# Value products of two neighbouring tiles in one run, in the second batch of an attention and feed-forward kernel

## The chip, the cores and the metric

The kernel runs on one core of one Trainium2 chip. Its time is that of one execution on the device, in microseconds (us); the number compared is the median of several runs. Before the change three runs gave 717.25, 718.96 and 721.09 us, a median of 718.96. One more execution was profiled, and every row below is of that one: it took 717.12 us, of which 715.3 us lie between the first and the last instruction of the program (the span).

A core has a matrix engine (PE, whose weight loads are shown apart as PEld), a vector engine (DVE), a scalar engine (ACT), a general engine (POOL) and a sync engine (SP) that here issues nearly all DMAs. Each engine takes its own instructions strictly in order.

## The reference

Three steps follow each other: attention in which a query sees only the keys of its own hash bucket, a feed-forward layer with x * sigmoid(x), and a second one with x - tanh(x). All in 32 bits.

```python
# q, k, v: (2, 8, 768, 64); proj: (64, 6)
q_bits = (np.einsum('bhsd,dk->bhsk', q, proj) > 0)       # k_bits likewise
q_bucket = np.sum(q_bits * 2 ** np.arange(6), axis=-1)   # k_bucket likewise
mask = q_bucket[:, :, :, None] == k_bucket[:, :, None, :]
scores = np.where(mask, scale * q @ k.T, -1e9)
attn = np.exp(scores - max); attn = attn / (sum + 1e-09)
x = (attn @ v), heads side by side                       # (1536, 512)
h = x @ w_in;   x = (h * sigmoid(h)) @ w_out             # 512 -> 2048 -> 512
h = x @ w_in2;  out = (h - tanh(h)) @ w_out2             # 512 -> 2048 -> 512
```

## The kernel before

**Attention.** There are 2 batches of 8 heads, and a head has 6 tiles of 128 queries against all 768 keys: 96 tiles, 48 of each batch. For each head q and k are split into a high and a low part (`q_hi`, `k_hi`, `q_lo`, `k_lo`; the low part of q is line L420, that of k L427) so that two short-format products give a 32-bit one; a product with `proj` (the hash, L454) gives the bucket bits, which are written into spare rows of the same operands, so that the scores come out masked. A tile then goes this way: four score matmuls (L658, `ps<-k,q`), the maximum on DVE (L662), the bias (L667) and the exponential on ACT (L672), a high half in 16 bits (L354, `hl<-p`) and a low half on POOL (L726, `hl<-p,hl`), one transposing DMA for both (L729, `pt<-hl`), and the value products: 18 matmuls of 65 columns (L750 to L752), for each of 6 key tiles high by high, high by low and low by high, all accumulated in one bank. Some tiles of the first batch are transposed on PE instead (L686), and seven of those use one 32-bit product (L744). When all 6 tiles of a head are done the result is divided by the sums (L773 to L781) and transposed (L793). The values v are scaled and split per pair of heads (L554 to L590, the helpers `copy` L354 and `scaled` L358 and L360).

**Feed-forward.** The hidden layer is done in four chunks of 512. Weights come as 64-bit words and are converted to 32 bits by ACT, POOL and DVE (first layer L1061 to L1083, second L1386 to L1401), then split in high and low. L1143 are the matmuls into the hidden layer, L1147 the tanh, L1151 the gate, L354 `gh` and L1158 its two halves, L1221 the matmuls out of it and L1226 to L1232 the accumulation. The first batch's tokens go through the first layer while the second batch's attention still runs: from about 124 us on PE alternates between score tiles, value products and groups of twelve feed-forward matmuls of 384 columns. After that comes the first layer for the second batch (16-bit operands, with weights read back from DRAM, L944 to L996), and then the second layer for all tokens, with seven products in place of eight (L1565, groups of six, with L1576 and L1582 putting them together, the gate in L1606 to L1616, the matmuls out of the hidden layer in L1656 and their accumulation in L1661 and L1663).

**What sets the order.** No instruction is issued where it is written. Every piece of work is handed to a planner (`Plan.add`) with the engines that may do it, an assumed cost on each, a key (roughly the moment at which it is due), the pieces that it depends on and the buffers that it takes. `Plan.order` then runs a list schedule: on each engine it takes, among the pieces that could start soonest, the one with the lowest key, and where several engines may do a piece a number `b_...` says how much later the first of them may be before the other is taken (50 or more: always the first). All these numbers stand in the table `KNOBS`. Pieces with the same `line` keep their sequence: score tiles `s`, value products `pv`, transposing DMAs `pt`, and sets of weight buffers `wset`. The value products of a tile get their key from `K["pv"]`; the list `two` already allows two tiles to be put into one piece, when `twos` is set and the batch is the second. The transposed probabilities have four buffers (`pt_slots`).

Of the kernel before, what the change touches and what calls it, by code (L numbers as in the profile page):

```python
# [25 lines left out]

KNOBS = dict(b_ysc=2.96, b_wsc=0.38, convw=36.631, cw=6, cjw=3.488, stt=0.005, hold_w2=20, twos=0, start=1.292,
             step=1.908, gap=9.852, step1=3.658, ffn=3.795, ffn3=2.276, pv=10.67, prep=15.957, hash=20.15,
             slack=0.056, conv=34.353, conv0=81.24, vld=4.608, vmax=5.066, vsplit=11.76, x2=0.165, direct=0.354,
             direct1=0, b_qh=100, b_qlo=2.34, b_kup=100, b_vlo=100, b_bi=100, b_thi=100, b_shi=100, b_slo=100,  # L30
             b_xh=2.01, b_xlo=100, b_wlo=100, b_clip=2.73, b_hhi=1.34, k_m=0.1, k_e=0.334, k_t=2.024, k_th=2.717,
             k_tl=1.55, k_hi=1.446, k_lo=1.897, k_f=2.576, cj=3.28, cl=7.627, ahead=2, emode=1, lmode=1, xsets=0,
             raws=8, vmax1=24.884, ffn2=1.46, xprep=20.673, xprep1=2.231, xk1=4.211, convo=55.136, convh=107.674,
             fill=8.355, convo0=43.254, convh0=58.847, fill0=36.161, plain=3, cj2=3.475, half=2, b_xph=2.35,
             b_xpl=100, b_cl2=2.82, b_wl2=100, b_sh=100, b_ss=100, b_u3=100, b_hh2=1.21, b_hl2=0.01, by=2.442,
             by2=7.875, parts=5.995, wend=46.5, b_part=2.81, vst1=5.174, vgap=6.028, vl=15.282, vsp=2.176,
             whole=0.17, chunk=0, b_kh=100, b_vh=0.38, b_vs=-0.33, b_whi=100, hold_r=30.482, hold_v=11.313,
             hold_v1=23.734, hold_w=10.65, hold_o=49.111, near=2)

# [169 lines left out]
def lsh_attention_moe_kernel(  # L209
# [180 lines left out]
    for n in range(NHEAD):  # L390
# [11 lines left out]
        else:  # L402
            ld = [add("SP", 0.4, lambda raw=raw, b=b, h=h: nc.sync.dma_start(out=get(raw), in_=qkT[b, h]), at - 12,
                      takes=[raw], tail=2.47, hold=at - K["hold_r"] if n > 1 else 0.0)] * 2
# [29 lines left out]
        parts = [qh, kh]  # L434
# [96 lines left out]
    for x in range(B * H // 2):  # L531
# [7 lines left out]
        if x == 0:  # L539
            la, va, hold_v = K["vld"], a0 + K["vmax"], K["hold_v"]  # L540
# [348 lines left out]
    for ps_i, (e, fresh, blks) in enumerate(PASSES):  # L889
# [4 lines left out]
        for c, fc in enumerate(chunks):  # L894
# [3 lines left out]
            for m in range(2):  # L898
# [114 lines left out]
                for j in range(fc if m else KD):  # L1013
# [77 lines left out]
                    else:  # L1091
# [5 lines left out]
                    x = add(("ACT", "POOL"), c2(0.62, 0.62), w_hi, kj + 2.5, [a] + prior[:1],  # L1097
                            takes=[held] if j == 0 else [], uses=[wa] + ([held] if j else []), give="whi")
                    y = add(("POOL", "DVE"), c2(1.29, 0.68), w_lo, kj + 3, [x], uses=[wa, held], port=("DVE",), give="wlo")
# [641 lines left out]
```

## Time and profile before

| | |
|---|---|
| runs | 717.25, 718.96, 721.09 us |
| profiled execution | 717.12 us, span 715.3 us |
| PE busy | 692.8 us, 97% of the span |
| DVE, ACT, POOL busy | 578.9 (81%), 481.3 (67%), 464.3 us (65%) |
| chain that ended last | PE 71%, DVE 14%, ACT 9% of the span |
| TensorE clock granted | 0.995 on average, 0.91 in the first 40 us |

Busy is the time in which an engine executes something, with the pipelined parts of consecutive instructions counted once. A matmul's shown duration is longer than the distance to the next one, because they overlap: distances between starts are what a list of matmuls costs. Time in which PE is idle shows only as the difference between a stretch and PE's busy time in it, and a weight load that nothing hides shows as a larger distance between two starts.

### The profile page before, as it was taken

How to read it: one execution, taken by the hardware profiler on the slowest of the kernel's cores; microseconds unless marked ns; L12 is line 12 of the kernel's file. 1: busy time of each engine (PE TensorE's matmuls, PEld its weight loads, DVE VectorE, ACT ScalarE, POOL GpSimd, SP SyncE). 2: the span in 40 equal slices, each digit the busy share in tenths (PEclk: the TensorE clock that was granted, in tenths of full speed). 3: DMA queues.
4: the chain of work that ended last, by engine and by line, in shares of the span. 5: the costliest groups of instructions: out<-in, count | busy, mean ns of one | idle time of the engine just before them, and what ended most of it. 6: DMA issues, size and time to landing. Idle time of an engine off the chain costs nothing.

```text
span 715.3 us, 14275 instructions
## 1 busy us (share of the span) xinstructions
PE 692.8 (97%) x5372; PEld 566.9 (79%) x5372; DVE 578.9 (81%) x1141; ACT 481.3 (67%) x884; POOL 464.3 (65%) x376
## 2 busy tenths in 40 slices
PE   7888899999999999999999999999999999999998
PEld 4777789999999999999655666558697796978977
DVE  5999999798797898778898758996689689786563
ACT  6799999997897896765866554655645546463250
POOL 6799998887688776845439482659855655772010
PEclk9899999999999999999999999999999999999999
DMA  9999998998999999993444004210033014110102
GB/s 326 225 234 246 209 199 178 257 221 198 220 237 267 218 210 230 236 198 97 150 147 158 16 1 133 89 59 1 1 94 127 17 59 122 57 60 1 58 31 89
DMA packets 148249, 101.48 MB, mean 142 GB/s; under 512 B 120668, under 2 KB 129116, under 8 KB 148180
## 3 DMA queue, kind: packets, MB, share of 16 engines
q1 hardware_dynamic: 147812, 100.27, 56.4%
q8 instruction: 42, 0.69, 0.4%
q10 hardware_dynamic: 368, 0.30, 0.1%
q14 instruction: 27, 0.22, 0.1%
HBM read 57.97 MB, written 11.53 MB: 97 GB/s over the span
## 4 chain that ended last, share of the span: by engine, by line
PE 71%; DVE 14%; ACT 9%; issue 3%; DMA 2%; POOL 1%; ACTq 0%; SPq 0%; DVEq 0%; POOLq 0%
PE psm L1656 18%; PE psm L1221 14%; PE psm L1143 12%; PE psm L1565 11%; PE ps L658 7%; ACT p L672 2%; PE pso L750 2%; PE pso L751 2%; PE pso L752 2%; PE ps L454 2%; DVE wcol L944 1%; DVE cv L1397 1%; DVE p L662 1%; ACT p L354 1%; DVE cv L1392 1%
## 5 line engine op out<-in xcount | busy, mean ns | idle before, releaser
L726 POOL TENSOR_TENSOR hl<-p,hl 128x768 f16<-128x768 f32 x75 | 126.0, 1682 | 37.3 <-ACT hl L354 31.7
L1565 PE MATMUL psm<-xoh,ws 128*128 128x384 f16 x448 | 113.2, 327 | 2.5 <-ACT x L1576 2.2
L1221 PE MATMUL psm<-gh,wh 128*128 128x384 f16 (+1 forms) x384 | 107.3, 332 | 0.0
L1565 PEld LDWEIGHTS <-ws 128*128 128x128 f16 x672 | 64.2, 98 | 47.1 <-issue 6.1
L662 DVE TENSOR_SCALAR_CACHE_REDUCE p<-ps 128x768 f32<-128x768 f32 x96 | 90.7, 951 | 12.0 <-PE ps L658 9.7
L658 PE MATMUL ps<-k,q 128*128 128x384 f32 x384 | 90.0, 361 | 6.9 <-DVE p L662 4.1
L672 ACT ACTIVATE p<-p,bi 128x768 f32<-128x768 f32 x96 | 89.8, 941 | 1.5
L1656 PE MATMUL psm<-gh,wh 128*128 128x384 f32 x256 | 88.5, 346 | 0.1
L1656 PE MATMUL psm<-gl,wh 128*128 128x384 f32 x256 | 85.9, 335 | 0.8 <-DVE gl L1616 0.8
L1656 PE MATMUL psm<-gh,wl 128*128 128x384 f32 x256 | 85.8, 335 | 0.0
L1221 PE MATMUL psm<-gl,wh 128*128 128x384 f32 (+1 forms) x256 | 84.7, 331 | 0.0
L658 PEld LDWEIGHTS ps<-k,q 128*128 128x128 f32 x384 | 65.6, 194 | 10.9 <-DVE p L662 7.2
L1565 PE MATMUL psm<-xol,ws 128*128 128x384 f16 x224 | 73.1, 326 | 0.0
L1143 PE MATMUL psm<-x16h,wh 128*128 128x384 f16 x256 | 63.4, 326 | 0.0
L354 ACT CAST hl<-p 128x768 f16<-128x768 f32 x75 | 62.7, 836 | 0.6
L1221 PEld LDWEIGHTS <-wh 128*128 128x128 f16 x384 | 37.4, 98 | 24.6
L1143 PEld LDWEIGHTS <-wh 128*128 128x128 f16 x384 | 37.2, 98 | 24.4
L1663 DVE TENSOR_TENSOR acc<-acc,psm 128x384 f32<-128x384 f32 x48 | 26.3, 550 | 32.8 <-PE psm L1656 32.8
L750 PE MATMUL pso<-v16h,pt 128*128 128x65 f16 x450 | 49.5, 195 | 0.0
L1656 PEld LDWEIGHTS psm<-gh,wh 128*128 128x128 f32 x256 | 48.1, 188 | 1.5 <-DVE acc L1663 0.2
L1656 PEld LDWEIGHTS psm<-gl,wh 128*128 128x128 f32 x256 | 48.1, 188 | 1.5 <-DVE gl L1616 1.5
L751 PE MATMUL pso<-v16l,pt 128*128 128x65 f16 x450 | 48.9, 194 | 0.0
(202 smaller groups left out, 2014.6 us busy)
## 6 DMA issues: line engine op xcount, KB each, us to landing
w<-in_w_in_dram SPq DMA_DIRECT2D x32, 512.0 KB
w<-in_w_out_dram SPq DMA_DIRECT2D x32, 512.0 KB
r<-in_qkT_dram SPq DMA_DIRECT2D x15, 768.0 KB
wi<-wa SPq DMA_DIRECT2D x16, 256.0 KB
wo<-wa SPq DMA_DIRECT2D x16, 256.0 KB
wl<-wi SPq DMA_DIRECT2D x16, 256.0 KB
wl<-wo SPq DMA_DIRECT2D x16, 256.0 KB
vr<-in_v_dram SPq DMA_DIRECT2D x8, 384.0 KB
```

Of the source, the lines that this page charges most:

```text
L354: nc.scalar.copy(out, in_) if e == "ACT" else ENG[e].tensor_copy(out, in_)
L658: nc.tensor.matmul(out=get(ps)[:, u, 0:HS], lhsT=x[:, t * 128:(t + 1) * 128], rhs=c[:, u * HS:(u + 1) * HS], start=(j == 0), stop=(j == 1))
L662: nc.vector.tensor_scalar(get_p().rearrange("p (c s) -> p c s", c=2), get(ps)[:, :, 0:HS], FLOOR, None, op0=ALU.max, op1=ALU.max, accum_ou ...
L672: nc.scalar.activation(out=get_p(), in_=get_p(), func=ACTF.Exp, scale=0.125, bias=get(bi))
L726: ENG[e].tensor_tensor(get_hl()[:, 1, :], get_p(), get_hl()[:, 0, :], op=ALU.subtract)
L750: nc.tensor.matmul(out=o, lhsT=pt[:, kt, :], rhs=v16[:, kt, :], start=(kt == 0), stop=False)
L751: nc.tensor.matmul(out=o, lhsT=pt[:, kt, :], rhs=v16l[:, kt, :], start=False, stop=False)
L1143: nc.tensor.matmul(out=ps, lhsT=a[:, k, fs], rhs=x_of(b_, blk)[:, k, :], start=(k == first and j == 0), stop=(k == last - 1 and j == 2))
L1221: nc.tensor.matmul(out=ps, lhsT=a[:, f, ds], rhs=b_.tile[:, f, :], start=(f == 0 and j == 0), stop=(f == fc - 1 and j == 2))
L1565: nc.tensor.matmul(out=ps, lhsT=sw[a][:, o, 2 * k + p, :], rhs=xw[b_][:, k, :], start=(first and k == 0 and j == 0), stop=(k == 1 and j == 2),
L1656: nc.tensor.matmul(out=ps, lhsT=a[:, f, ds], rhs=b_.tile[:, f, :], start=(f == 0 and j == 0), stop=(f == F - 1 and j == 2))
L1663: nc.vector.tensor_tensor(acc_tile(), acc_tile(), get(bk)[:, 0:NB], op=ALU.add)
```

## The change

`twos` goes from 0 to 1: in the second batch the value products of tiles 1 and 2, 3 and 4, 5 and 6 of a head are one piece of 36 matmuls, which becomes due with the second tile and depends on the probabilities of both. 27 further numbers of the table are new, most of them due times that differ by a few us at most. Those that move work between engines: `b_qlo` 2.34 to 100 (low parts of q and k always on POOL), `b_hhi` 1.34 to 100 (high half of the first layer's gate always on ACT), `b_sh` 100 to 1.04 (high halves of the second layer's weights may go to DVE), `b_part` 2.81 to -0.21 and `b_hl2` 0.01 to -0.14. Besides, the first piece of a set of converted weights now keeps the sequence of `wset`.

```diff
-... twos=0, start=1.292, ... conv0=81.24, vld=4.608, ... b_qlo=2.34, ...
+... twos=1, start=1.405, ... conv0=79.02, vld=4.346, ... b_qlo=100, ...
...
                     x = add(("ACT", "POOL"), c2(0.62, 0.62), w_hi, kj + 2.5, [a] + prior[:1],
-                            takes=[held] if j == 0 else [], uses=[wa] + ([held] if j else []), give="whi")
+                            takes=[held] if j == 0 else [], uses=[wa] + ([held] if j else []), give="whi",
+                            line=None if j else "wset")
```

The lines that `twos` switches were there before:

```python
            two.append((1.32 if whole else 0.56, pv, ready + (vready32 if whole else vready), keep))
            if not K["twos"] or b == 0 or len(two) == 2:
                def products(fs=tuple(x[1] for x in two)):
                    for f in fs:
                        f()
```

All of the order comes out anew. In the changed kernel's rows the lines from L1099 on carry a number that is one higher.

PE, second batch, before: the end of one tile's value products (`pt_3954` are its transposed probabilities) and what follows.

```order
L751 LDWEIGHTS pt_3954
L751 MATMUL pso_4097<-v16l_141,pt_3954 128x65
L752 LDWEIGHTS pt_3954
L752 MATMUL pso_4097<-v16h_140,pt_3954 128x65
L658 MATMUL ps_4119<-k1_2993,q1_2991 128x384 x2
L658 MATMUL ps_4119<-k2_2994,q2_2992 128x384 x2
L1143 MATMUL psm_4127<-xh0_78,wh_3733 128x384
L1143 MATMUL psm_4127<-xl0_80,wh_3733 128x384
```

PE, second batch, changed: the end of the first tile's products of a pair (`pt_3809`).

```order
L751 LDWEIGHTS pt_3809
L751 MATMUL pso_3762<-v16l_141,pt_3809 128x65
L752 LDWEIGHTS pt_3809
L752 MATMUL pso_3762<-v16h_140,pt_3809 128x65
L750 LDWEIGHTS pt_3849
L750 MATMUL pso_3762<-v16h_140,pt_3849 128x65
L751 LDWEIGHTS pt_3849
L751 MATMUL pso_3762<-v16l_141,pt_3849 128x65
```

Where scores or feed-forward matmuls stood between two tiles, the second tile (`pt_3849`) now follows at once.

DVE near the start, as a difference (`k_228` and `k_229` belong to the third head, `vstat` to the scaling of v).

```order
 L385 TENSOR_TENSOR hw<-x_82,hw 64x82
 L662 TENSOR_SCALAR p,mx<-ps 128x768 x2
-L427 TENSOR_TENSOR k_228<-r,k_229 128x768
+L554 TENSOR_REDUCE vstat<-vr 128x1
+L555 TENSOR_SCALAR vstat<-vstat 128x1
 L501 TENSOR_SCALAR q_202<-ps,cst_sb 18x768
 L503 TENSOR_SCALAR k_204<-ps,cst_sb 18x768
```

The low part of k of the third head leaves DVE for POOL, and the maximum of v comes earlier.

DVE at the end of the first feed-forward, before: the last low half of its gate (L1158), the accumulations (L1232) and the first pieces of the second layer (L1582, L1609).

```order
L1158 TENSOR_TENSOR gl<-psm,gh 128x384
L1401 SCALAR_TENSOR_TENSOR wa<-w,cv 128x512
L1609 SCALAR_TENSOR_TENSOR x_82<-psm,vsum,x_82 128x384
L1392 TENSOR_SCALAR cv<-wa 128x512
L1582 TENSOR_TENSOR psm<-psm,x_82 128x384
L1397 SCALAR_TENSOR_TENSOR cv<-w,cv 128x512
L1232 SCALAR_TENSOR_TENSOR acc<-psm,wsum,acc 128x384
L1401 SCALAR_TENSOR_TENSOR wa<-w,cv 128x512
L1609 SCALAR_TENSOR_TENSOR th<-psm,vsum,th 128x384
L1582 TENSOR_TENSOR psm<-psm,x_82 128x384
L1232 SCALAR_TENSOR_TENSOR acc<-psm,wsum,acc 128x384
```

DVE at the same place, changed (L1159, L1233, L1583 are the former L1158, L1232, L1582, and L1276 reduces the result).

```order
L1152 SCALAR_TENSOR_TENSOR psm<-th,psm 128x384
L1583 TENSOR_TENSOR x_82<-psm,x_82 128x384
L1233 SCALAR_TENSOR_TENSOR acc<-psm,wsum,acc 128x384
L1393 TENSOR_SCALAR cv<-x_82 128x512
L1159 TENSOR_TENSOR gl<-psm,gh 128x384
L1398 SCALAR_TENSOR_TENSOR cv<-w,cv 128x512
L1233 SCALAR_TENSOR_TENSOR acc<-psm,wsum,acc 128x384
L1402 SCALAR_TENSOR_TENSOR x_82<-w,cv 128x512
L1276 TENSOR_REDUCE ycol<-acc 128x1
```

The accumulations of the last chunk now stand ahead of nearly all of the second layer's first gates. On PE this is two product groups of six, then the last eight groups of the first layer, then 13 product groups, where it was nine, then the eight, then four, before the first matmul of L1656.

## Rows read from the trace of the kernel before

**Rows 1.** Busy us and count of each engine by stretch, then clock and DMA.

```profile
0.00:40.00 40.00, 32.67 (x204) 23.10 (x204) 31.04 (x62) 29.09 (x52) 29.13 (x27) 0.91 0.92 265
40.00:120.00 80.00, 72.69 (x899) 64.59 (x899) 76.86 (x169) 78.28 (x150) 74.65 (x53) 1.00 0.98 213
120.00:360.00 240.00, 240.00 (x2194) 220.12 (x2193) 200.57 (x402) 191.79 (x351) 169.76 (x129) 1.00 0.93 212
360.00:500.00 140.00, 135.75 (x828) 87.23 (x827) 116.03 (x230) 83.44 (x147) 87.23 (x71) 1.00 0.22 72
500.00:700.00 200.00, 199.88 (x1185) 160.31 (x1185) 150.54 (x275) 98.71 (x187) 103.50 (x99) 1.00 0.17 56
700.00:715.30 15.30, 11.82 (x69) 11.49 (x67) 3.88 (x8) 0.00 (x0) 0.00 (x0) 1.00 0.28 104
```

**Rows 2.** PE in order of time, 217 to 222 us: start, duration, instruction.

```profile
217.17 0.95 PE L658 MATMUL ps<-k,q 128*128 128x384 f32 x4
217.96 0.20 PE L750 MATMUL pso<-v16h,pt 128*128 128x65 f16 x1
...
218.53 0.42 PE L1221 MATMUL psm<-gh,wh 128*128 128x384 f32 x1
218.78 0.34 PE L1221 MATMUL psm<-gl,wh 128*128 128x384 f32 x1
...
220.69 0.39 PE L454 MATMUL ps<-q,hw 128*82 128x512 f32 x1
...
221.74 0.34 PE L1221 MATMUL psm<-gh,wh 128*128 128x384 f32 x1
```

**Rows 3.** Weight loads at the same place.

```profile
218.47 0.10 PEld L752 LDWEIGHTS <-pt 128*128 128x128 f16 x1
218.50 0.19 PEld L1221 LDWEIGHTS psm<-gh,wh 128*128 128x128 f32 x1
```

**Rows 4.** The 87th tile in order of time: PE, POOL, SP, PE.

```profile
276.73 0.60 PE L658 MATMUL ps<-k,q 128*128 128x384 f32 x2
...
280.89 1.66 POOL L726 TENSOR_TENSOR hl<-p,hl 128x768 f16<-128x768 f32 x1 [0.59 <-POOL wa L1064]
...
282.58 1.44 SPq L729 DMA_TRANSPOSE pt<-hl  x1
...
287.85 0.20 PE L750 MATMUL pso<-v16h,pt 128*128 128x65 f16 x1
```

**Rows 5.** Groups by line: instruction, count, busy us, mean ns, idle before.

```profile
L427 DVE TENSOR_TENSOR k<-r,k 128x768 fp32r<-128x768 f32 x6 | 9.1, 1520 | 5.6 <-ACT k L358 5.6
L1064 DVE TENSOR_SCALAR wa<-wa 128x512 f32<-128x512 f32 x5 | 3.9, 772 | 0.4 <-ACT wa L1061 0.3
L360 DVE TENSOR_SCALAR vr<-vr,vstat 128x768 f32<-128x768 f32 x1 | 1.5, 1537 | 0.0
L360 DVE TENSOR_SCALAR x<-vr,vstat 128x768 f32<-128x768 f32 x1 | 1.4, 1427 | 0.0
L427 POOL TENSOR_TENSOR k<-r,k 128x768 fp32r<-128x768 f32 x10 | 18.4, 1838 | 0.7 <-ACT k L358 0.6
L1061 ACT ACTIVATE wa<-w 128x512 f32<-128x512 f32 x32 | 21.3, 673 | 0.8 <-DMA w<-in_w_out_dram 0.8
L354 ACT CAST q<-r 128x768 fp32r<-128x768 f32 (+1 forms) x24 | 20.0, 831 | 2.9 <-POOL wa L1064 1.8 <-DMA r<-in_qkT_dram 0.9 <-PE ps L658 0.2
L358 ACT ACTIVATE k<-r,cst_sb 128x768 fp32r<-128x768 f32 x16 | 15.0, 934 | 2.0 <-DMA cst_sb<-in_cst_dram 2.0
```

**Rows 6.** Busy time by stretch, as in rows 1, from 435 to 484 us.

```profile
435.00:484.00 49.00, 46.26 (x283) 28.65 (x281) 47.25 (x95) 29.65 (x54) 22.97 (x24) 1.00 0.32 103
```

**Rows 7.** Who PE waited for after 340 us: total us, times, longest.

```profile
PE psm L1565 <- ACT x L1576: 2.2, 3, 0.9
PE psm L958 <- DVE wcol L955: 0.8, 1, 0.8
PE psm L1656 <- DVE gl L1616: 0.8, 1, 0.8
```

**Rows 8.** The chain that ended last, merged: start, us, what.

```profile
500.34 12.69 PE psm L1565 x78
```

More of the change, by code (lines that the diff above doesn't have):

```diff
@@ L25 @@
 W_MAX = 2.0 ** 16 * (1.875 - 2.0 ** -23)
[L27 to L38, printed above, removed]
@@ new lines @@
+KNOBS = dict(b_ysc=2.96, b_wsc=0.46, convw=37.137, cw=6, cjw=3.488, stt=0.005, hold_w2=20, twos=1, start=1.405,
+             step=1.908, gap=9.852, step1=3.658, ffn=3.795, ffn3=2.305, pv=10.67, prep=15.957, hash=20.218,
+             slack=0.056, conv=34.353, conv0=79.02, vld=4.346, vmax=5.066, vsplit=11.76, x2=0.165, direct=0.354,
+             direct1=0, b_qh=100, b_qlo=100, b_kup=100, b_vlo=100, b_bi=100, b_thi=100, b_shi=100, b_slo=100,
+             b_xh=2.01, b_xlo=100, b_wlo=100, b_clip=2.73, b_hhi=100, k_m=0.076, k_e=0.334, k_t=2.024, k_th=3.627,
+             k_tl=1.55, k_hi=1.446, k_lo=1.897, k_f=2.576, cj=3.28, cl=7.191, ahead=2, emode=1, lmode=1, xsets=0,
+             raws=8, vmax1=24.884, ffn2=1.46, xprep=20.673, xprep1=2.231, xk1=4.211, convo=56.316, convh=107.674,
+             fill=8.355, convo0=44.343, convh0=57.522, fill0=34.117, plain=3, cj2=3.553, half=2, b_xph=2.35,
+             b_xpl=100, b_cl2=2.64, b_wl2=100, b_sh=1.04, b_ss=100, b_u3=100, b_hh2=0.81, b_hl2=-0.14, by=2.442,
+             by2=7.562, parts=5.964, wend=46.5, b_part=-0.21, vst1=5.27, vgap=6.028, vl=15.282, vsp=2.176,
+             whole=0.17, chunk=0, b_kh=100, b_vh=0.38, b_vs=-0.33, b_whi=100, hold_r=29.758, hold_v=11.313,
+             hold_v1=23.734, hold_w=10.682, hold_o=49.111, near=2)
```

## The prediction

> **What bounds the kernel now.** I read three views: the busy times by stretch, PE's order of time at two places, and the waits of PE. The first says most. PE is busy for 240.00 of 240.00 us between 120 and 360 us and for 199.88 of 200.00 between 500 and 700 [rows 1]: there the kernel is as long as PE's own list of matmuls, and nothing that another engine does is worth anything unless it makes PE wait. The clock is the higher of its two levels in all stretches but the first (0.91 in 0 to 40 us, 1.00 after). PE stands idle in three places: 7.33 us in 0 to 40, 7.31 us in 40 to 120, 4.25 us in 360 to 500; the 3.48 us at the end are the last result on its way out. From 40 to 120 us ACT is busy for 78.28 of 80 us, DVE for 76.86, POOL for 74.65: the softmax of the first batch runs on three engines that are nearly full, ACT most of all, and PE waits for them. So a change can gain time in three ways: fewer or cheaper matmuls in the full stretches, less work on the fullest engine before 120 us, or shorter waits between 360 and 500 us.
>
> **Terms that I sum.** All durations are of the profiled execution, which took 717.12 us (span 715.3 and 1.8 around it); the median of the three runs is 718.96, so I take the sum off both.
>
> Part 1, value products in pairs. PE executes the same matmuls. What falls away is the change of kind after each run of value products. In the trace scores start at 217.17, the value products of a tile follow at 217.96, and the first feed-forward matmul at 218.53: 0.57 us for 18 products. Its second matmul comes at 218.78, 0.25 us later, while from there to 220.69 eleven matmuls take 1.91, or 0.174 each [rows 2]: 0.08 lost after the run. The four score matmuls before, which also follow a run of value products, take 0.79 where 4 x 0.174 is 0.69: 0.10 lost. I take 0.09. The weight load shows why: the load for the first matmul of 384 columns begins at 218.50, just behind the last load of the value products, and lasts 0.19, and no matmul long enough lies over it [rows 3]. PE's order has 48 runs of value products in the second batch before and 24 after, 33 in the first batch both times, and while the second batch is done PE is never idle: 24 x 0.09 = 2.2 us gained. The ends are 24 x 0.08 = 1.9 and 24 x 0.10 = 2.4.
>
> The Trainium skill (TensorE: Matmul & The Clock Gate, Step-by-step: what each phase is for) says that PE pulls the next weight load ahead of matmuls in flight, so that it runs beside them. By that rule the change of kind costs nothing and this term is 0. The trace agrees inside a run of one kind and not at its end.
>
> The pair has a price: PE stops at the second tile until its probabilities have come back through POOL and the transposing DMA. How much time the new order leaves for this is added up from PE's order in the changed kernel with starts of [rows 2] (scores 0.69, a group of twelve 2.08, a tile's products 0.57, a hash 1.05). From the start of the second tile's scores to its products it leaves 11.9 us in the tightest of the 24 pairs (four scores, three groups, a pair, the first tile's products, a hash), 12.9 to 13.6 in seven, 14.0 or more in the rest. In the trace the tightest tile had 11.1: scores at 276.73, POOL's low half until 282.55, the DMA issued until 284.02, products at 287.85 [rows 4], and PE was not idle there. So I cost the wait at nothing.
>
> Part 2, work moved before PE is full. I count what stands on each engine before the 49th tile's softmax. DVE loses two low parts of k at 1.52, and two scalings of v at 1.54 and 1.43, and gains two clips of a weight at 0.77: 4.5 us less. ACT gains two high halves of v (128x768, not seen there before; the nearest row is the 0.93 of k) and one absolute value at 0.67, and loses one cast of q at 0.83 and one scaling of k at 0.93: 0.8 us more. POOL gets the two parts of k at 1.84, 3.7 us, before smaller moves that take some off again [rows 5]. Were DVE the pace, the start would be 4.5 us shorter; were POOL, 3.7 longer. ACT is nearest to full, it has 0.8 more, and less waiting for DVE can give that back out of its 1.72 idle us. I take 0 and keep both ends. The loads move too: on SP the first weight's load now stands behind one more load of v and one more of q and k; the head of that queue is as it was, and with DVE busy for 31.04 of the first 40 us [rows 1] I cost this at nothing. The other 3 low parts of k move from DVE to POOL after 120 us, where POOL is busy for 169.76 of 240 us: hidden.
>
> Part 3, the change to the second feed-forward. From 435 to 484 us (from the gate of the 57th of the 64 gate groups of the first feed-forward to the first copy of a result of the second) DVE is busy for 47.25 of 49.00 us and PE for 46.26 [rows 6]: DVE is the pace, and PE's waits there are for copies of ACT (2.2 us in three) and for the low halves of DVE [rows 7]. The new order puts the eight accumulations of the last chunk ahead of seven products of the next layer. DVE's work between these two points stays: its instructions, each at its mean of the trace, come to 52.8 us before and 53.5 after, both with their overlap. PE has one group of six more in that time (78 such matmuls take 12.69 us from 500.34 on [rows 8], so six take 1.0) that it need not do later, against DVE's 0.7: 0.3 gained. The wait at the run of nine products can go, because the copy now has eight output groups to finish behind; at DVE's pace that is mostly given back. I take 0.5 gained, between all 4.25 idle us gone and as much again lost.
>
> Part 4, fixed engines. Six high halves of the gate go from DVE to ACT, six halves of the second layer's weights and three partial sums from ACT to DVE, and eight small instructions to POOL, all after 120 us. They lie under PE's full stretches, and after 500 us POOL is busy for 103.50 of 200 and DVE for 150.54: nothing. The wait edit in the weight conversion only fixes the order in which weight buffers are taken: nothing.
>
> Sum: 2.2 + 0 + 0.5 = 2.7 us gained. 717.12 - 2.7 = 714.4 for such an execution, 718.96 - 2.7 = 716.3 for the median.
>
> **Rivals.**
> First, the early stretch gets shorter. DVE's 4.5 us count, because ACT's idle time before 120 us (10.91 in the first stretch, 1.72 in the second) is waiting for DVE, and ACT pays its 0.8. Speaking for it: DVE is within 4% of full. Against: ACT within 3%. Time: 716.3 - 4.5 + 0.8 = 712.6. To its chance I add that of all waits between 360 and 500 us gone: 718.96 - 2.2 - 4.25 = 712.5.
>
> Second, the early stretch gets longer: POOL with 3.7 more, in the same queue as the low halves of the probabilities, holds tiles back. For it: 74.65 of 80 us. Against: POOL waits for others there and its other moves take off work. Time: at most 716.3 + 3.7 = 720.0.
>
> Third, the load is hidden after all and the pairs bring nothing: 718.96 - 0.5 = 718.5. Against it speaks every one of the rows above.
>
> Fourth, slower: the pairs wait. POOL has five more low parts of k in its queue by the end of attention, 9.2 us; if scores to landed probabilities take longer than they did at 276.73, PE stops at the second tile in order, and everything behind it, the feed-forward of the first batch too, stops with it. With 13.0 us for that way the pairs wait 1.4 us in all, with 13.5, 4.1, with 14.0, 8.1 (sums of what is missing to the distances above). At 14.0 the median is 716.3 + 8.1 = 724.4; it is slower than before by more than 0.5% from about 13.8, 2.7 us above the shortest way seen. For it: the way is queueing on three engines and SP. Against: POOL has 70 idle us in that stretch.
>
> **How the numbers follow.** A measurement of this kernel tells about 0.5%, 3.6 us, from no change. The forecast as summed: 0.45, its own range 713 to 719, of which 0.13 lies more than 3.6 below 718.96 and 0.32 within. Early stretch shorter or the later waits gone: 0.27, all faster. Early stretch longer: 0.09, within. Load hidden: 0.03, within. Pairs wait: 0.16, slower. So faster 0.40, the same 0.44, slower 0.16. The range goes from 710, below which lies some tenth that both of the faster cases come together, to 722, above which lies most of the fourth rival.
>
> **What would show it.** Part 1: 57 runs of value products, 24 of them in the second batch with 36 products each, the loss after each still 0.08 to 0.10, and some 2 us less from PE's first full microsecond to the end of attention. If PE shows idle time before L751 or its loads between 130 and 330 us, the fourth rival holds. Part 2: the 49th score group starts within a microsecond or two of its place before, and PE's idle time before 120 us stays near 14.6. Part 3: PE's idle time between 360 and 500 us near 4, no wait at the first run of products of the second feed-forward. I am wrong if PE's idle time before 120 us moves by more than 3 us, since that one term has nothing but full engines under it.

## The result, and the profile after

The changed kernel takes 722.79 us (median of 12 runs, 718.56 to 727.48), the kernel before 717.55 in 12 runs of the same chips. The ratio is 1.0069, with a 95% interval of 1.0053 to 1.0085: 5.0 us slower (3.8 to 6.1), where 2.7 us faster was forecast. The profiled execution took 722.84 us, its span is 720.9 us, 5.6 more than that of before.

The busy times by stretch, with the columns of [rows 1]:

```profile
0.00:40.00 40.00, 30.85 (x184) 20.96 (x185) 29.61 (x57) 27.98 (x48) 27.64 (x25) 0.87 0.87 244
40.00:120.00 80.00, 73.77 (x880) 65.26 (x881) 75.33 (x172) 77.85 (x151) 76.27 (x55) 1.00 1.07 223
120.00:360.00 240.00, 236.67 (x2209) 220.58 (x2208) 194.85 (x392) 192.59 (x353) 175.41 (x133) 1.00 0.92 209
360.00:500.00 140.00, 134.04 (x819) 83.94 (x818) 112.29 (x230) 82.23 (x147) 83.77 (x70) 1.00 0.24 78
500.00:700.00 200.00, 200.00 (x1190) 161.25 (x1189) 151.16 (x271) 93.86 (x177) 115.20 (x109) 1.00 0.17 56
700.00:720.90 20.90, 17.41 (x99) 16.71 (x97) 8.66 (x17) 2.98 (x6) 0.00 (x0) 1.00 0.21 76
```

PE is busy for as long as before (692.75 us in all, 692.81 before). What grew is its idle time: from 7.33 to 9.15 us in the first 40, from nothing to 3.33 us between 120 and 360, and from 4.25 to 5.96 between 360 and 500; from 40 to 120 us it fell from 7.31 to 6.23. The stretch that was full in [rows 1] is full no longer.

Where the time went is read best at equal work. For the table I gave each matmul the median distance to the next one of its kind in the trace of before, and added these up along PE's order. A cell says how many us later than before PE had done the work that before had done at the time on the left. The columns other than the first are experiments that follow below.

| before, us | changed | numbers_alone | pairs_only | old_to_57 | reads_first | late_spread |
|---|---|---|---|---|---|---|
| 115 | 1.41 | 0.20 | 0.55 | -0.44 | -0.29 | -0.41 |
| 130 | 1.79 | 0.54 | 0.56 | -0.47 | 0.09 | -0.03 |
| 155 | 3.93 | 2.29 | 1.09 | -0.46 | 2.21 | 2.11 |
| 260 | 2.73 | 2.16 | 0.42 | -1.53 | 1.00 | 0.91 |
| 275 | 3.89 | 2.23 | 0.17 | -0.39 | 2.15 | 2.05 |
| 340 | 4.11 | 2.43 | -0.43 | -0.76 | 1.86 | 1.90 |
| 375 | 5.75 | 2.14 | -0.43 | 0.94 | 2.46 | 3.34 |
| 405 | 5.49 | 1.77 | 0.69 | 0.89 | 2.46 | 5.43 |
| 500 | 5.94 | 3.69 | 0.94 | 1.24 | 2.82 | 5.80 |
| end | 5.61 | 3.36 | 0.80 | 0.91 | 2.49 | 5.48 |

Down the first column: 1.8 us are lost by 130 us, 2.1 between 130 and 155, 1.2 won back from 155 to 260, 1.2 lost at 269 (by the changed kernel's clock), 1.6 lost between 360 and 375, and little after that.

The first 1.8 us are not shown to come from the order: nine kernels of the experiments have the same order as the changed one on PE, DVE, ACT and POOL up to 118 us, and at 115 us they stood between 2.1 us ahead of before and 0.2 behind, where the changed one stood 1.4 behind. The step from 1.77 to 3.69 in the second column is a fall of the clock in that execution, which the last section shows.

**The part won back** is the pairs. This is PE in order of time at one pair (start, duration, instruction), against [rows 2]:

```profile
264.25 0.21 PE L750 MATMUL pso<-v16h,pt 128*128 128x65 f16 x1
...
265.37 0.95 PE L658 MATMUL ps<-k,q 128*128 128x384 f32 x4
266.16 0.34 PE L1144 MATMUL psm<-xh,wh 128*128 128x384 f32 x1
```

36 products take 1.12 us, and the four score matmuls behind take 0.79 where 0.69 would do: the same 0.10 lost as before, once for two tiles. Nearly all runs of products after 125 us lose 0.08 to 0.10 when they end (ahead of a hash 0.04); there are 29 such ends, where before had 53. From 155 to 260 us there are 14 pairs: 14 x 0.09 = 1.3, and the table shows 1.2.

**130 to 155 us.** PE in order of time again; in brackets the idle time ahead of an instruction and who ended it:

```profile
144.20 0.94 PE L658 MATMUL ps<-k,q 128*128 128x384 f32 x4
144.98 0.49 PE L793 MATMUL psm<-cst_sb,xt 128*128 128x128 f32 x3
146.29 0.97 PE L658 MATMUL ps<-k,q 128*128 128x384 f32 x4 [0.82 <-DVE p L662]
...
149.22 0.87 PE L658 MATMUL ps<-k,q 128*128 128x384 f32 x4
151.36 0.44 PE L1144 MATMUL psm<-xh,wh 128*128 128x384 f32 x1 [1.28 <-DVE gl L1159]
```

DVE at the same place:

```profile
145.27 0.96 DVE L662 TENSOR_SCALAR_CACHE_REDUCE p<-ps 128x768 f32<-128x768 f32 x1 [0.56 <-PE ps L658]
...
150.76 0.55 DVE L1159 TENSOR_TENSOR gl<-psm,gh 128x384 fp32r<-128x384 f32 x1
```

In the second batch there is one buffer for scores, called the score bank below: the kernel gives the other one up (`shut = Held((s_slots[1],))`) before the first feed-forward starts. So the score tile of 146.29 can't start until DVE has read out that of 144.20. Only three small matmuls stand between the two. The other wait is for a bank of the hidden layer, freed by DVE's last step of its gate. By the distances between starts the two waits are 0.99 and 1.44 us, somewhat more than in brackets; the experiments below are told in such distances. No engine is full there. The busy times from 130 to 155 us, first before, then changed:

```profile
130.00:155.00 25.00, 25.00 (x261) 23.32 (x260) 21.35 (x41) 23.21 (x45) 20.20 (x15) 1.00 1.06 232
```

```profile
130.00:155.00 25.00, 22.90 (x233) 21.12 (x230) 20.76 (x41) 21.18 (x39) 20.58 (x14) 1.00 1.04 235
```

**269 us.** A hash, which uses the same bank, follows a score tile at once. PE, and under it DVE's read-out of that tile:

```profile
268.25 0.86 PE L658 MATMUL ps<-k,q 128*128 128x384 f32 x4
270.25 0.43 PE L454 MATMUL ps<-q,hw 128*82 128x512 f32 x1 [1.15 <-ACT gh L354]
```

```profile
269.14 0.96 DVE L662 TENSOR_SCALAR_CACHE_REDUCE p<-ps 128x768 f32<-128x768 f32 x1 [0.72 <-PE ps L658]
```

The bracket names ACT, but a hash doesn't need what ACT wrote there; the read-out ends at 270.10 and the hash starts 0.15 us later, as the tile at 146.29 started 0.06 us after the read-out of the tile before it (145.27 + 0.96). The wait is 1.31 us by distance. The pair stands behind the hash. In the order of before a tile's products, a group of twelve and another tile's products stood between:

```profile
265.51 0.86 PE L658 MATMUL ps<-k,q 128*128 128x384 f32 x4
266.21 0.21 PE L750 MATMUL pso<-v16h,pt 128*128 128x65 f16 x1
...
266.77 0.42 PE L1221 MATMUL psm<-gh,wh 128*128 128x384 f32 x1
...
268.96 0.20 PE L750 MATMUL pso<-v16h,pt 128*128 128x65 f16 x1
...
269.51 0.44 PE L454 MATMUL ps<-q,hw 128*82 128x512 f32 x1
```

**360 to 500 us.** SP's queue (issues of transfers) in the changed kernel, then in the kernel before:

```profile
343.67 12.40 SPq L1381 DMA_DIRECT2D w<-in_w_in_dram  x2
356.15 0.38 SPq L941 DMA_DIRECT2D wl<-wo  x1
359.41 0.33 SPq L1381 DMA_DIRECT2D w<-in_w_in_dram  x1
359.79 2.20 SPq L941 DMA_DIRECT2D wl<-wo  x3
```

```profile
340.03 0.50 SPq L941 DMA_DIRECT2D wl<-wo  x1
354.29 0.33 SPq L1380 DMA_DIRECT2D w<-in_w_in_dram  x1
```

A load of second-layer weights waits on SP for a free buffer, and the reads of first-layer weights (`wl<-wo`) stand behind it. Three of the four are issued at 359.79, 5 us later than before (where they follow the load of 354.29). PE is 4.1 us late by then, so at equal work the reads are late by 1.0 us. PE's waits after 340 us, against [rows 7]:

```profile
PE psm L958 <- DVE wcol L955: 2.3, 2, 1.7
PE psm L1566 <- ACT x L1577: 1.8, 1, 1.8
PE psm L1657 <- ACT gh L354: 1.0, 1, 1.0
PE psm L1657 <- DVE gl L1617: 0.9, 1, 0.9
```

The first line is the small matmul that spreads the largest weight: 0.8 us before, 2.3 now.

**The start.** The granted clock (third column from the right) from 26 us on, changed kernel:

```profile
26.00:28.00 2.00, 1.42 (x6) 0.80 (x5) 1.97 (x5) 2.00 (x4) 2.00 (x2) 0.60 0.41 76
28.00:30.00 2.00, 2.00 (x8) 1.40 (x7) 1.90 (x7) 1.72 (x4) 2.00 (x3) 0.50 0.88 334
30.00:32.00 2.00, 2.00 (x24) 1.93 (x24) 1.70 (x3) 0.88 (x3) 2.00 (x2) 0.50 1.59 285
32.00:34.00 2.00, 2.00 (x14) 1.84 (x14) 1.16 (x1) 1.87 (x4) 0.88 (x1) 0.69 0.80 173
```

It is at the lower of its two levels (0.50, 1.2 GHz) until 33 us; before, it was back at 1.00 at 30 us:

```profile
28.00:30.00 2.00, 2.00 (x7) 1.89 (x7) 1.76 (x3) 2.00 (x4) 2.00 (x3) 0.53 1.08 201
30.00:32.00 2.00, 2.00 (x30) 1.96 (x30) 1.97 (x7) 1.31 (x5) 2.00 (x2) 1.00 0.55 161
```

In both it fell between 26 and 28 us. Ahead of that PE was busy for only 0.22 us between 22 and 24 (0.58 before), and from 26 to 28 for 1.42 (2.00 before); that this kept it down for longer is not shown.

### The profile page after: what moved, and what is told of

It reads as the page before. It is cut to its first block, busy times and chain, and to the rows that moved or that the text cites. A ratio compares the mean times of both kernels' runs of the same rounds, so it can differ in the third digit from the quotient of the medians.

```text
span 720.9 us, 14277 instructions
## 1 busy us (share of the span) xinstructions
PE 692.7 (96%) x5372; PEld 568.7 (79%) x5372; DVE 571.9 (79%) x1134; ACT 477.5 (66%) x878; POOL 478.3 (66%) x389
## 4 chain that ended last, share of the span: by engine, by line
PE 70%; ACT 9%; DVE 9%; DMA 5%; POOL 3%; issue 2%; SPq 0%; ACTq 0%; DVEq 0%; POOLq 0%
PE psm L1657 18%; PE psm L1566 13%; PE psm L1144 12%; PE psm L1222 12%; PE ps L658 6%; PE ps L454 2%; DMA wl<-wi 2%; ACT p L672 2%; PE pso L750 2%; PE pso L751 2%; PE pso L752 2%; DMA pt<-hl 1%; ACT hl L354 1%; ACT wh L354 1%; DVE p L662 1%
## 5 line engine op out<-in xcount | busy, mean ns | idle before, releaser
L658 PE MATMUL ps<-k,q 128*128 128x384 f32 x384 | 87.8, 354 | 4.6 <-DVE p L662 3.9
L1657 PEld LDWEIGHTS psm<-gh,wl 128*128 128x128 f32 x256 | 48.1, 188 | 0.0
L750 PE MATMUL pso<-v16h,pt 128*128 128x65 f16 x450 | 47.2, 195 | 0.0
```

Of the source, the lines that this page charges most:

```text
L658: nc.tensor.matmul(out=get(ps)[:, u, 0:HS], lhsT=x[:, t * 128:(t + 1) * 128], rhs=c[:, u * HS:(u + 1) * HS], start=(j == 0), stop=(j == 1))
L750: nc.tensor.matmul(out=o, lhsT=pt[:, kt, :], rhs=v16[:, kt, :], start=(kt == 0), stop=False)
L1657: nc.tensor.matmul(out=ps, lhsT=a[:, f, ds], rhs=b_.tile[:, f, :], start=(f == 0 and j == 0), stop=(f == F - 1 and j == 2))
```

## The experiments

In all but two of them a given list of pieces per engine takes the place of the planner's choice, so that all engines keep the order of before, or of the changed kernel, and only the pieces named move (buffers are chosen as they come free). Each was timed in five rounds against the kernel before on the same chip; the ratio is to that, and differences between two experiments are taken from their ratios.

**pairs_only.**

```diff
 PE, order of before, for each pair of the second batch
-products of tile 1 ... products of tile 2
+... products of tile 1, products of tile 2
```

> The order of the kernel before on every engine, with one thing moved on PE: in the second batch the products of tiles 1, 3 and 5 of a head stand directly ahead of those of tiles 2, 4 and 6. If pairing only saves the change of kind (24 x 0.09 us), PE stays without idle time from 130 to 330 us and the kernel is 2.2 us faster than before, about 715.4. If pairing makes PE wait, because the products that were moved stood between two score tiles and gave DVE and ACT time, PE shows idle time ahead of score or feed-forward matmuls between 130 and 330 us (3.3 us in the changed kernel) and the time is 717.5 to 719.5, no gain or a loss of up to 2 us.

Ratio 0.9980 (0.9964 to 0.9996): 1.4 us faster (0.3 to 2.6). PE from 120 to 360 us:

```profile
120.00:360.00 240.00, 239.58 (x2200) 221.88 (x2199) 203.43 (x402) 192.39 (x351) 169.55 (x130) 1.00 0.93 212
```

0.42 us idle. Pairs alone gain, and the 2.2 us that were forecast for them lie within the interval. In the table 0.54 us go between 130 and 155, 1.5 come from there to 340, and 1.1 go again by 405, at a wait of 2.11 us for the spread of the largest weight at 380 us (0.99 before).

**split_again.** The opposite, in the order of the changed kernel.

```diff
 PE, order of the changed kernel, for each pair
-score tile ... products 1, products 2
+products 1, score tile ... products 2
```

> The order of the changed kernel, with the products of the first tile of each pair moved back up on PE, ahead of the last score group before the pair. If the waits of 0.99, 1.44 and 1.32 us that PE has at 145, 150 and 269 us in the changed kernel come from the pairs, they go (3.75 us) and the changes of kind come back (2.2 us): about 1.5 us faster than the changed kernel. If they come from the order of the other engines, they stay, and the kernel is 2.2 us slower than the changed one, about 725.

Ratio 1.0237 (1.0206 to 1.0268). This doesn't decide what it was meant for: in the last head the moved products stand ahead of their probabilities, and PE waits 6.0 us for two transposing DMAs and 2.4 us for the result of the head before. Up to 290 us the three waits were 0.99, 0.80 and 1.31 us: only the second shrank (from 1.44), ahead of which products had been moved.

**old_start and new_start.**

```diff
-all pieces in one order
+pieces planned ahead of the 49th score tile: order of before (old_start) or changed (new_start)
+the rest: the other order
```

> The order of the kernel before for all pieces planned ahead of the 49th score tile, and the order of the changed kernel for the rest. In the two traces PE's losses differ by 1.3 us at 120 us and by 1.9 at 130 us. If the beginning is one of the causes, this kernel is 1.3 to 1.9 us faster than the changed one, about 721, and the granted clock of the first 40 us is back at 0.91 from 0.87. If the differences of the beginning are given back later (they were 3 us at 40 us and 0.1 at 95 us), it stays at 722.8.

> The reverse: the order of the changed kernel for all pieces planned ahead of the 49th score tile, and the order of before for the rest. If the beginning is a cause: 1.3 to 1.9 us slower than before, about 719.2. If it is given back: 717.5.

Ratios 1.0055 (1.0035 to 1.0075) and 1.0046 (1.0025 to 1.0067). The old start takes off 1.0 us of the 5.0, which these intervals can't tell from nothing. In new_start 2.2 us are a wait for a hash at 130 us, where the two orders meet, so it doesn't show what the start costs; at 115 us its PE was 0.3 us ahead of before. Section "Not expected" has what the runs together show.

**fill_gaps.**

```diff
 PE, order of the changed kernel
-score tile, 3 transposes, score tile, feed-forward 2 x 3
+score tile, 3 transposes, feed-forward 2 x 3, score tile
-score tile, feed-forward 3, pair        (149 us)
+score tile, pair, feed-forward 3
-score tile, hash, pair                  (269 us)
+score tile, pair, hash
```

> The order of the changed kernel with three moves on PE alone: at 144 us two feed-forward pieces of three matmuls (1.04 us) go between two score tiles that stood 0.24 us apart; at 150 us the pair of products goes ahead of the feed-forward piece that waited; at 269 us the pair of products goes between the last score tile and the hash that followed it at once. In the second batch there is one score bank, and its next user must wait about 1.3 us after a score tile until the maximum has been read out on DVE. If missing filler between the users of that bank is the cause, the waits of 0.99 and 1.32 us go and that of 1.44 us shrinks by 1.1: about 3 us faster than the changed kernel, 719.8. If the waits come from DVE's own backlog, they move to the next place and the time stays at 722.8.

Ratio 1.0053 (1.0034 to 1.0071), 1.2 us less than the changed kernel, not 3, and not told apart from it by these intervals. At 144 and 149 us the waits of 0.99 and 1.44 us became 1.18, 0.60, 0.42 and 0.29, now mostly for the hidden layer's banks. At 269 us the hash waits no longer, but the second tile of the pair ahead of it does, 0.55 us for its transposing DMA; and 0.61 came up at 289, at a score tile. Its bank was read out late on DVE, behind a weight conversion that had waited for POOL:

```profile
287.93 0.69 DVE L1067 TENSOR_SCALAR cv<-wa 128x512 int32<-128x512 int32 x1 [1.05 <-POOL wa L1064]
288.53 0.95 DVE L662 TENSOR_SCALAR_CACHE_REDUCE p<-ps 128x768 f32<-128x768 f32 x1
```

The gaps had only been moved.

**reads_first.**

```diff
 SP, order of the changed kernel
-load w_in, read wo 1, load w_in, read wo 2 to 4
+read wo 1, load w_in, read wo 2 to 4, load w_in
```

> The order of the changed kernel with one move on SP alone: four reads of first-layer weights stand again ahead of the two loads of second-layer weights that wait on SP for a free buffer (from 344 to 356 us and until 359 us). If this blocking is the cause of PE's wait of 1.90 us at 366 us, the wait goes: 1.5 us faster than the changed kernel, 721.3. If the wait follows the data's way through DRAM or DVE's queue, it stays, at 722.8.

Ratio 1.0027 (1.0011 to 1.0043). PE's wait at 366 us:

```profile
PE psm L958 <- DVE wcol L955: 0.7, 1, 0.7
```

0.7 against 1.7 us: a good half of it was SP's blocking. In the table 0.6 us are lost from 340 to 375, where the changed kernel lost 1.6. The rest of its gain lies ahead of 130 us, where nothing was moved: it is the start, which differs from run to run.

**fill_and_reads** is both.

> Both: the three moves on PE and the one on SP in the order of the changed kernel. If both causes hold and add up, 4.5 us faster than the changed kernel, 718.3, as fast as the kernel before. If what is gained in the second batch is given back later, 720 or more.

Ratio 1.0044 (1.0028 to 1.0059), 720.81 us: they don't add up.

**pairs_and_reads.**

```diff
 PE as in pairs_only; SP, order of before
-load w_in, read wo 2 to 4 ... load w_out, read wi 1, load w_out, read wi 2 to 4
+read wo 2 to 4, load w_in ... read wi 1 to 4, load w_out, load w_out
```

> The order of the kernel before with the pairs (as in the run that moved only them), and on SP seven reads of first-layer weights ahead of the loads of second-layer weights that wait for a buffer at 354, 370 and 372 us. If the waits of 1.0 to 2.1 us that PE has at 380 us in the orders of before come from that blocking, they go: 1.0 us faster than pairs alone, 2.4 us faster than before, about 716. If they don't: 717.

Ratio 0.9971 (0.9957 to 0.9985), 715.70 us: 2.1 us faster than before. The wait at 380 us is 0.72 us, where pairs_only had 2.11.

**first_pair_early.**

```diff
 PE, order of the changed kernel
-score tile (144), ... score tile (149), feed-forward 3, products 1, products 2
+score tile (144), products 1, ... score tile (149), products 2, feed-forward 3
```

> The order of the changed kernel with the first pair alone taken apart on PE: the products of its first tile go right behind the score tile at 144 us, those of its second behind the score tile at 149 us, both into places where PE waits (0.99 and 1.44 us). If what is missing there is any piece that needs neither a score bank nor a feed-forward bank, each wait shrinks by the 0.57 us of a tile's products: about 1.1 us faster than the changed kernel. If the engines behind are simply late by then, as the fill_gaps run suggests (there the wait only moved from the score tile to the feed-forward piece), PE waits as long in the next place and nothing is gained.

Ratio 1.0057 (1.0037 to 1.0078). The first wait shrank from 0.99 to 0.39 us, by the products' 0.57. But the second tile's products then waited 1.57 us for their transposing DMA. So what is ready there fills PE's gap, but little is ready.

**old_to_57.**

```diff
-old_start: the old order up to the 49th score tile
+the old order up to the 58th score tile
```

> The order of the kernel before for all pieces planned ahead of the 58th score tile (some 10 tiles into the second batch), the order of the changed kernel for the rest. If the 2.2 us that every kernel with the new order there loses between 130 and 155 us come from how the pieces between the 49th and the 58th tile stand, they go: at 155 us PE's loss is that of before, and the kernel is about 2 us faster than the one with the old order to the 49th tile (722.0), some 720. The savings of 20 pairs (1.8 us), the wait at 269 us (1.2), the late reads (1.5) and 0.5 after 450 us stay: 1.5 us slower than before. If the loss comes from engines that the new start leaves behind, it was there with the old start too, and so shouldn't; then nothing changes against that kernel.

Ratio 1.0016 (1.0003 to 1.0029), 719.44 us: 2.8 us less than old_start. In the table nothing is lost between 130 and 155 us any more, and in the waits nothing is left from there:

```profile
PE psm L958 <- DVE wcol L955: 2.4, 3, 1.4
PE ps L454 <- ACT gh L354: 1.1, 1, 1.1
```

These are all of its PE's waits from 120 to 400 us: what is left is the hash at 269 us and the late reads.

**switch_alone and numbers_alone** leave the order to the planner.

```diff
 switch_alone: kernel before
-twos=0
+twos=1        (and line="wset" as in the change)
 numbers_alone: changed kernel
-twos=1
+twos=0
```

> The kernel before with the switch for pairs alone and the kept sequence of weight buffers that the planner then needs; all other numbers are the old ones, and the planner orders everything anew. In its order two users of the one score bank follow each other directly once (a score tile behind a hash, late in the second batch) and once with 0.54 us between them. If pairs save 0.08 to 0.09 us each and such neighbours cost up to 1.3 us, it is about 1 us faster than before, 716.7; if the rest of the order matters more than either, it can be anywhere between 715 and 721, and what it gains or loses is then the planner's.

> The changed kernel with the switch for pairs back at 0: the other new numbers alone, the planner orders everything anew. In its order no two users of the score bank stand closer than 0.82 us. If the pairs cause the waits of the second batch, those (3.3 us) go and the changes of kind come back (2.2 us): about 1 us faster than the changed kernel. If pairs only save, it is 2.2 us slower, 725.

Ratios 1.0004 (0.9987 to 1.0020) and 1.0026 (1.0012 to 1.0040). With the old numbers the planner's order with pairs is as fast as before. In it PE waits twice ahead of the second tile of a pair for its transposing DMA (0.43 and 0.95 us by distance), and once for the score bank, where a score tile stands directly behind another:

```profile
265.83 0.96 PE L658 MATMUL ps<-k,q 128*128 128x384 f32 x4
267.87 0.97 PE L658 MATMUL ps<-k,q 128*128 128x384 f32 x4 [1.08 <-DVE p L662]
```

With the new numbers, the kernel is 3 us faster without pairs. In the table the changed kernel loses 3.7 us from 130 to 405 and numbers_alone 1.2. PE's waits in numbers_alone from 120 to 340 us:

```profile
PE psm L1144 <- DVE gl L1159: 1.3, 1, 1.3
PE ps L658 <- DVE p L662: 0.3, 1, 0.3
```

The wait at 269 us is gone (products, a group of twelve and products stand between the two users again), that at 150 is not: of the 2.1 us between 130 and 155 some 1.8 are there without pairs. The wait at 366 us is gone too, though SP blocks there in the same way (13.34 us): the small matmul stands 12 matmuls later on PE.

**late_spread.**

```diff
 PE, order of the changed kernel, at 366 and 384 us
-spread (L958), 12 matmuls
+12 matmuls, spread
```

> The order of the changed kernel with one small matmul moved on PE at two places: the one that spreads the largest weight (L958) goes 12 matmuls later, at 366 and at 384 us. It stands in front of matmuls that could run, while DVE has not yet found that maximum. If its place is what costs, the waits of 1.90 and 0.74 us go and the kernel is 2.0 to 2.6 us faster than the changed one, about 720.5. If the weights that hang on it come too late then, PE waits at the next groups instead, and nothing is gained.

Ratio 1.0043 (1.0028 to 1.0059). PE's waits from 340 to 420 us:

```profile
PE psm L958 <- DVE wcol L955: 4.1, 4, 1.6
```

At 367 us it waits 0.67 us in place of 1.91, but 1.74 us at the next such place, 399 us, and more at the ones around. The wait moved on again.

**hash_early.**

```diff
 PE, order of the changed kernel
-score tile (149), feed-forward 3, pair, feed-forward 3, hash
+hash, pair, feed-forward 3, score tile (149), feed-forward 3
```

> The order of the changed kernel with the hash that stands at 153.7 us moved up on PE, together with the first pair of products, ahead of the score tile of 149 us (and its reading out on DVE ahead of that tile's maximum). In the order of before the hash and a tile's products stand there (1.6 us). If what PE lacks at 150 us is work that is ready, the wait of 1.44 us goes: 1.4 us faster than the changed kernel. If the engines are late by then, the wait appears at the score tile or the feed-forward piece behind.

Ratio 1.0066 (1.0040 to 1.0092). PE there:

```profile
150.45 0.97 PE L658 MATMUL ps<-k,q 128*128 128x384 f32 x4 [1.13 <-DVE hb L509]
...
153.04 0.44 PE L1143 MATMUL psm<-xh,wh 128*128 128x384 f32 x1 [1.10 <-DVE gl L1158]
```

The wait of 1.44 us became two of 1.28 and 1.26 (to the score tile and to the feed-forward piece behind). PE has more to do and waits the longer: the read-outs on DVE stand behind the gates there, in order.

**mended.**

```diff
 order of before to the 58th score tile, then the changed one, with reads_first and late_spread
```

> The order of before to the 58th score tile, the changed one behind it, with the reads ahead of the blocked loads on SP and the small matmul 12 later at two places. Left of the changed order are 20 pairs, the hash directly behind a score tile at 269 us (1.2 us) and 0.5 us after 450 us. If the causes named so far are all, this comes to 719.4 - 1.6 - 0.9, about 717, a little faster than before. If something else costs as well, it stays at 719.

Ratio 1.0007 (0.9991 to 1.0024): as fast as before. A wait of 1.74 us came up at 396 us.

**pairs_best.**

```diff
 pairs_and_reads; PE at 380 us
-spread (L958), 12 matmuls
+12 matmuls, spread
```

> The fastest kernel so far (the order of before with pairs and with the reads ahead of the blocked loads, 715.7) with the small matmul at 380 us 12 matmuls later. If its wait there (0.72 us) goes, about 715.0, 2.7 us faster than before; if not, 715.7.

Ratio 0.9959 (0.9946 to 0.9973): 2.9 us faster than before, the fastest of all; it is not told apart from pairs_and_reads. The wait of 0.72 us is gone, and one of 0.77 came up at 393 us.

## Why the prediction was wrong

**The step that failed** is the first one: that PE is as long as its own list between 120 and 360 us, so that nothing another engine does is worth anything there unless it makes PE wait. This is what [rows 1] show for the order of before. I carried it over to an order that was new throughout, looked for one wait only, that of a pair for its own probabilities, costed it at nothing, and took the changes of kind as the whole of the stretch. The changed kernel's PE is idle there for 3.33 us, nearly all of it in three places (145, 150 and 269 us), none of which is in the sum.

**Part 1, the saving,** held: the ends of runs still cost 0.08 to 0.10 us, there are 24 fewer of them, and the pairs alone in the old order gain 1.4 us (0.3 to 2.6) where I had 2.2, which the interval holds. The rival that the load is hidden, which the Trainium skill's rule (TensorE: Matmul & The Clock Gate, Step-by-step: what each phase is for) spoke for, fell with the same rows.

**Part 1, the price of pairs,** I took as the wait of a pair for its own probabilities, and costed it at nothing. In the changed kernel PE never waits ahead of products between 130 and 330 us, so that was right, and the fourth rival, which had the sign, had the wrong place (it is there in other orders: 0.43 and 0.95 us in switch_alone, 0.55 in fill_gaps). The price was elsewhere. Products and feed-forward groups stood between two users of the one score bank, and gave DVE the time to read it out. With pairs the planner put the next user at once behind the last (269 us, 1.2 us in the table), and did so again with the old numbers (switch_alone, 1.24 us at 266 us); without pairs, in before and numbers_alone, it did not. A pair by itself does not cost this: in pairs_only the group of twelve still stands between, and nothing waits there. A look at PE's order for such neighbours, which I had in hand, would have shown it. In fill_gaps, with the pair put in between, part of the time went to the pair's own wait, and part came up 20 us later.

**Part 2** ended where I stopped counting, at the 49th tile. The next nine tiles, where the first batch ends and the feed-forward starts, cost 2.1 us; old_to_57 shows that it is the order of these pieces. Mostly it is not the pairs (numbers_alone keeps 1.8). Three edits of PE's order there (fill_gaps, first_pair_early, hash_early) moved the waits on and took little away, which points to what stands on DVE, ACT and SP behind it; DVE itself was idle for PE three times between 143 and 148 us (0.43, 0.56 and 0.59 us), so the two engines wait for each other in turn. Which of the 27 numbers made it so is open. For the start itself I took 0 between -4.5 and +3.7; by old_start it is some 1 us, which the intervals can't tell from nothing, and PE's idle time before 120 us moved by 0.7 us, within what I had named.

**Part 3**: 0.5 us gained was forecast, 0.45 us are lost between 405 and 500 us, within the bounds (1.9 to 2.3 in other executions, where the clock fell there). The wait of [rows 7] at the runs of products went from 2.2 us in three to 1.8 in one, and two for ACT's and DVE's halves came up (1.0 and 0.9), where there had been one of 0.8.

**Not in the sum at all** was SP after 340 us. I followed SP's queue at the start and not here, where a load moved ahead of four reads. PE lost 1.6 us; with the reads ahead a good half of it goes, with the small matmul later it moves to the next such place. What the other half hangs on is open.

**Part 4**: nothing was forecast, and 0.33 us were gained after 500 us.

That the profiled execution's 5.6 us lie so near the 5.0 of the ratio is in part chance: 1.4 of them were lost by 115 us, where eight of nine other executions with the same order up to there were ahead of before.

## What to carry to other kernels

A stretch in which the bounding engine is never idle says that its present order leaves the others enough time, not that they have time to spare: when the order changes, look at every pair of neighbours that share one bank, and at what stands behind a blocked transfer. Joining two short pieces to save a change of kind can take away the filler that stood between others, so it is best tried with the rest of the order held fast (1.4 us gained here) and not with a scheduler that orders everything anew (nothing gained in switch_alone, where the pairs were the only new number). A wait that an edit removes is gained only if the time at equal work, some stretches later, is still gained: in fill_gaps, late_spread and hash_early the waits only moved to the next place.

## Not expected of the hardware

One score bank sets a distance of 2.0 to 2.1 us from score tile to next user: 144.20 to 146.29, 268.25 to 270.25, and 265.83 to 267.87 in switch_alone (0.9 us of matmuls, 0.96 us of read-out, and the signals between them). The Trainium skill (Perfetto Trace Analysis, Matmuls) asks for independent groups of matmuls to go round different PSUM banks, so that the read-out of one lies beside the next group; the rows above show what it costs where the next user stands directly behind on one buffer, and no run here had two in that stretch.

The granted clock splits the runs of one and the same kernel. Of 60 runs with the changed order on all engines or with a few pieces of it moved by hand (without split_again, all 6 of whose runs are on the low side), 30 had a mean granted clock of 0.993 or less, and took 2.5 us more than the other runs of their kernel (median). With the new order for the start alone it was 4 of 12 runs, with the new order for the rest alone 6 of 32, with the old order throughout and pairs 0 of 36, and 5 of 104 runs of the kernel before. That is (0.50 - 0.05) x 2.5, an estimate of 1.1 us on average for the new order. One kernel is an exception: in numbers_alone it was 6 of 10, and they took no longer. The fastest run of the changed kernel, 718.56 us, had 0.998, the slowest, 727.48, had 0.991, and the profiled one 0.993.

A mean doesn't say where the clock was low, but the profiled executions do, and it is not at the start alone. There it was between 0.87 and 0.96 over the first 40 us. In numbers_alone, fill_gaps and mended it fell to its lower level once more near 488 us, in the passage to the second feed-forward, and in split_again at the same place of its order, 504 us:

```profile
485.00:490.00 5.00, 3.18 (x10) 2.60 (x9) 3.30 (x5) 1.89 (x5) 5.00 (x4) 0.73 0.01 3
```

This is numbers_alone; the changed kernel has 1.00 there. Between 405 and 500 us these four lost 1.9 to 2.3 us, the eight others with the new order in that place 0.35 to 0.45. In all twelve PE waits three times around there (1.96, 1.1 and 1.1 us by distance). The order of before has shorter waits there (0.9, 0.4 and 0.9 us), and none of the six profiled executions with it showed such a fall. What decides whether the clock falls was not tried, nor what in the new order makes its runs differ.
